# Packed attention and SoLU: w_out's column sums on TensorE from the shifted bits, a fourth load buffer, and units placed anew

## The chip, the cores and the metric

One core of a Trainium2 chip runs the kernel. The metric is the device time of one execution in microseconds (us); lower is better. Beside whole executions there is one execution under the profiler, with the busy time of each engine: PE (TensorE), PEld (its weight loads), DVE (VectorE), ACT (ScalarE), POOL (GpSimd) and SP (SyncE, which here issues the DMAs).

## The reference

A two-step attention over packed queries p (8 batches, 8 heads, 576 rows, 64 columns a head, 32 packed rows) is followed by a layer with a SoLU and a norm:

```
def sm_attn(qq, kk, vv):
    s = scale * np.matmul(qq, kk.transpose(0, 1, 3, 2))
    s = s - np.max(s, axis=-1, keepdims=True)
    a = np.exp(s)
    a = a / (np.sum(a, axis=-1, keepdims=True) + 1e-09)
    return np.matmul(a, vv)
p_packed = sm_attn(p, k, v)
out = sm_attn(q, p_packed, p_packed)
...
x = out.transpose(0, 2, 1, 3).reshape(B * S, H * D)        # 4608 x 512
h = x @ w_in                                               # 512 x 1024
e = np.exp(h - h_max)
sm = e / (np.sum(e, axis=-1, keepdims=True) + 1e-09)
solu = h * sm
...
ln = (solu - mu) / np.sqrt(var + 1e-06) * g_ln
return (ln @ w_out).astype(np.float32)                     # 1024 x 512
```

w_in, w_out and g_ln enter through their raw words: w_in and w_out come as pairs of 32-bit words (64-bit floating point), which the kernel joins into float32 itself.

## The kernel before, in words

The work has two parts. The **setup** turns w_in into float32 and w_out into two float16 parts (wch and wcl, whose sum carries more digits than one). The **main part** goes over eight batches b; a batch has four tiles of 128 rows, and each pair of batches a fifth, shared one.

For each batch, `pack(b)` (L342 on) loads k and v, transposes k, forms the scores of p, a softmax and the packed rows `ppT`. `unpack(b)` (L419 on) transposes q, forms its scores against `ppT`, a softmax over blocks of 32, and z, the product of the packed rows with w_in, as a high and a low part (`zh`, `zl`; L485 to L500); the attention's weights also become a high and a low part (`a2h`, `a2l`; L507, L508). In batch 0 the low part of z is made from a copy by ACT (L491) and a difference on POOL (L493); in later batches by one DVE step (L500).

For each tile, `mlp_in` forms h with 12 matmuls (24 for the shared tile; L521), its maximum on DVE (L523), the exponential on ACT (L531) and u on DVE (L534). `mlp_norm` makes `negmu` on POOL (L542), the two float16 parts `yhl` on ACT (L544) and DVE (L545), and a transposing DMA on SP's queue to `yT` (L547); tiny steps on POOL (L551 to L555) end in the row factor. `mlp_out` has 24 matmuls per tile (L564) with wch and wcl, and a DVE step (L566); SP stores the tile (L571).

In the setup, `high_part` (L195 on) takes a chunk's upper words: a pass on ACT scales them (L202, into a buffer 'e' of which there are two), DVE shifts the bits left by three and drops the sign (L204), and DVE puts the sign back (L205). `add_low_part` (L207 on) brings in the lower words, in the way that `HOW` names for each of eight chunks (0 to 3 of w_in, 4 to 7 of w_out, of 1024 columns each): a power from DVE (L212); then either one DVE step (L217; ways 0, 2, 6) or an ACT pass (L220) and a product on POOL (1, 3) or DVE (4, 5) (L221); then the sum on POOL (1, 2, 4) or DVE (0, 5) (L233), or on PE (3, 6), where each half is a float32 matmul (L226) and a float32r one (L227), with a copy by ACT (L229, or L231, which also multiplies by g).

`prepare_w_out` (L284 on) also needs the sum down each column of g times the magnitude of w_out. For each of eight pieces of 512 columns ACT makes g times the absolute value of the high part (`mag`, float32r; L301), and a matmul with ones adds it to one PSUM tile (L302). From the sum DVE makes a power of two for each column (L307 to L311). Then each piece is multiplied by g (ACT, L321, where that has not been done), by the scale (L322, on the engine that `SCALED_BY` names: p for POOL, otherwise DVE), copied to float16 (L323, ACT) and its rest made (L330, on the engine of `REST_BY`). The pieces lie in the buffers that `yT` and `yhl` use later. The first `mlp_out` needs all pieces.

The order of the setup and batch 0 comes from a scheduler with a planned time for each instruction; `tc.high_priority(offset=...)` moves a group ahead or back, and lists such as `PACK0`, `W_IN`, `UNPACK0`, `W_OUT`, `PARTS`, `FIRST_BATCH` hold those offsets. From batch 1 on, PE keeps the order of the program, in which `LATER` tells how many units of `pack` and `unpack` stand between a tile's steps; the other engines still go by priorities. Each engine runs its own queue in order. `keep_busy` (L251 on) puts filler matmuls (L255) into PE's queue, as many as `BUSY` says. `LOADS` is the order of the first loads on SP's queue: w a chunk of w_in, o one of w_out, p and P the first and the remaining part of p, k, v, q those of batch 0. The large load buffers `raw` (three) serve k, q and two chunks of w_out in turn.

Of the kernel before, what the change touches and what calls it, by code (L numbers as in the profile page):

```python
# [21 lines left out]
PACK0 = [-350, 400, 2010, 365, -1000, 60, -2800, 200, 200]
W_IN = [[110, -260], [-3000, -210], [100, -3010], [20, 850]]
UNPACK0 = [-80, 350, -35, -110, -70, -25, 1965, 1025, 0]
W_OUT = [[190, -10, 1910], [20, -60, -925], [-50, 2000, 0], [3010, -385, -3000]]
SCALE_AT = -1060
CHUNKS = [6, 0, 7, 5, 1, 3, 4, 2]
PARTS = [100, -1160, -990, -200, -3010, -1050, 200, 200]
FIRST_BATCH = [[0, 0, 1, 1, 1, 2, 0, 2, 0, 2, 0, 0], [0, 1, 0, 0, 0, 4, 1, 1, 0, 0, 1, 1], [3, 0, 6, 0, 0, 0, 0, 0, 0, 0, 0, 0], [1000, 375], [0, -400, -50], 190]
# [9 lines left out]
def packed_attention_solu_kernel(ctx: ExitStack, tc: tile.TileContext, q: bass.AP, k: bass.AP, v: bass.AP, p: bass.AP, w_in: bass.AP, w_out: bass.AP, g_ln: bass.AP, out: bass.AP):  # L39
# [202 lines left out]
    minus_h = const.tile([P, P], F16, name='minus_h')  # L242
    nc.vector.tensor_scalar_mul(minus_h, ident, -1.0)
    minus_r = const.tile([P, P], F32R, name='minus_r')
    nc.vector.tensor_scalar_mul(minus_r, ident, -1.0)
# [38 lines left out]
    def prepare_w_out():  # L284


        wg = []
        mps = ps_o.tile([P, DM], F32, name='po')
        for n in range(NFC // 2):
# [5 lines left out]
            with tc.high_priority(offset=W_OUT[n][0]):  # L295
                anchor = high_part(wg[n], w_out_raw[n], 4 + n)
            with tc.high_priority(offset=W_OUT[n][1]):
                for i in range(2):
# [2 lines left out]
                    nc.scalar.activation(mag, wg[n][:, i * DM:(i + 1) * DM], AF.Abs, scale=g_sb[:, c:c + 1])  # L301
                    nc.tensor.matmul(mps, lhsT=ones, rhs=mag, start=c == 0, stop=c == NFC - 1)  # L302
            with tc.high_priority(offset=W_OUT[n][2]):
                add_low_part(wg[n], w_out_raw[n], 4 + n, g_sb[:, 2 * n:2 * n + 2])
        with tc.high_priority(offset=SCALE_AT):
# [5 lines left out]
            last = nc.vector.tensor_scalar_mul(inv, power, 2.0 ** (-14))  # L311
        for c in CHUNKS:
            with tc.high_priority(offset=PARTS[c]):
# [10 lines left out]
                if REST_BY[c] == 'e':  # L324
                    ps = ps_a.tile([P, 512], F32, name='pa')
                    nc.tensor.matmul(ps, lhsT=ident, rhs=w, start=True, stop=False)
                    nc.tensor.matmul(ps, lhsT=minus_h, rhs=wch[:, c], start=False, stop=True)
                    nc.scalar.copy(wcl[:, c], ps)
                else:
                    EN(nc, REST_BY[c]).tensor_tensor(out=wcl[:, c], in0=w, in1=wch[:, c], op=ALU.subtract)  # L330
        return last.ins
# [87 lines left out]
    def unpack(b):  # L419
# [57 lines left out]
        for n in range(2):  # L477
# [6 lines left out]
            for r, pz in enumerate(banks):  # L484
                nc.scalar.copy(z_h[:, r, cols], pz)  # L485
                if b == 0:
                    if ZL_BY[2 * n + r] == 'd':
                        nc.vector.tensor_tensor(out=z_l[:, r, cols], in0=pz, in1=z_h.bitcast(F32)[:, r, cols], op=ALU.subtract)
                    else:
                        z = mlp.tile([P, 512], F32, name='o_sb', bufs=2)  # L490
                        nc.scalar.copy(z, pz)  # L491
                        if ZL_BY[2 * n + r] == 'p':
                            nc.gpsimd.tensor_tensor(out=z_l[:, r, cols], in0=z, in1=z_h.bitcast(F32)[:, r, cols], op=ALU.subtract)  # L493
                        else:
                            rest = ps_a.tile([P, 512], F32, name='pa')
                            nc.tensor.matmul(rest, lhsT=ident, rhs=z, start=True, stop=False)
# [193 lines left out]
```

## Time and profile before

| | |
|---|---|
| time, three runs | 471.25 us (median; 470.44 to 472.5) |
| the profiled execution | 472.61 us, span 470.8 us |
| granted clock of PE, mean | 0.967 of full speed |
| PE busy | 430.8 us (92% of the span) |
| DVE busy | 350.5 us (74%) |
| ACT busy | 232.3 us (49%) |
| POOL busy | 147.1 us (31%) |
| first output matmul (L564) | at 108.9 us |
| DMA | 67.0 MB, mean 142 GB/s |

The span runs from the first to the last instruction. Busy times are sums over one execution; the idle time of an engine costs something only where the end waits for it. A row of a group gives the line, the engine, the operation with out<-in, the count, the busy time, the mean of one in ns, and then the idle time of the engine just before and what ended it. A row of one line's or tile's instructions gives the shortest, median and longest duration in ns, and the first and last start in us. A row of the timeline or of the chain that ended last begins with the start and the duration in us.

### The profile page before, as it was taken

Reading aid. Unit: us, or ns where it says so; the run is one execution under the profiler, and the core shown is the slowest. Engines: PE = TensorE matmul, PEld = TensorE weight load, DVE = VectorE, ACT = ScalarE, POOL = GpSimd, SP = SyncE. Lnnn points to the kernel's source line nnn. Section 1 sums busy time; section 2 is a strip of 40 time slices with the busy share of each in tenths; the row PEclk is TensorE's granted clock in tenths of the full one; section 3 lists DMA queues with packets and bytes.
Section 4 is the critical chain, followed back from the end, with each engine's and each line's share of the span. In section 5 each row is a group of like instructions: output and inputs, shape, how many; then the busy total and the mean of one; then the engine's idle time right before and its main releaser. Section 6 shows DMA issues by size and latency. Waiting matters only on the chain.

```text
span 470.8 us, 8265 instructions
## 1 busy us (share of the span) xinstructions
PE 430.8 (92%) x3116; PEld 234.4 (50%) x3116; DVE 350.5 (74%) x648; ACT 232.3 (49%) x404; POOL 147.1 (31%) x244
## 2 busy tenths in 40 slices
PE   9698695859979999999999999999999989999995
PEld 7472243633534555446644654566446536575552
DVE  3568979778769887997489879984898587655551
ACT  3577748654344463546245544562447344433430
POOL 3424656936103311431124114310332142211220
PEclk9979859888999999999999999999999999999999
DMA  9999998999579979968949495447233413525342
GB/s 257 338 274 290 149 205 118 130 208 148 104 151 173 165 120 202 159 140 137 220 71 165 98 206 101 98 100 173 51 84 68 92 45 90 112 67 130 73 101 77
DMA packets 237880, 67.00 MB, mean 142 GB/s; under 512 B 208912, under 2 KB 231440, under 8 KB 237328
## 3 DMA queue, kind: packets, MB, share of 16 engines
q1 hardware_dynamic: 237840, 66.48, 74.2%
q8 instruction: 24, 0.39, 0.4%
q14 instruction: 16, 0.13, 0.1%
HBM read 37.23 MB, written 9.44 MB: 99 GB/s over the span
## 4 chain that ended last, share of the span: by engine, by line
PE 42%; DVE 28%; POOL 7%; ACT 6%; issue 6%; DMA 6%; SPq 5%; DVEq 0%; ACTq 0%; POOLq 0%
PE po L564 21%; PE h L521 12%; DVE nm L523 4%; DMA zh<-in_moe_w_in_dram 3%; DVE u L534 3%; DVE qT L428 3%; DVE kT L350 3%; PE pa L407 3%; DVE yhl L545 2%; DVE zl L500 2%; ACT yhl L544 2%; SPq L134 2%; DMA raw<-in_k_dram 2%; ACT e L381 1%; DVE a2l L508 1%
## 5 line engine op out<-in xcount | busy, mean ns | idle before, releaser
L564 PE MATMUL po<-wch,yT 128*128 128x512 f16 x576 | 178.2, 380 | 1.2 <-DMA yT<-yhl 1.2
L564 PEld LDWEIGHTS <-yT 128*128 128x128 f16 x864 | 80.9, 98 | 113.0 <-issue 18.4
L564 PE MATMUL po<-wcl,yT 128*128 128x512 f16 x288 | 108.7, 379 | 0.0
L521 PE MATMUL h<-zh,a2h 128*128 128x512 f32 x160 | 69.3, 433 | 1.7 <-DVE u L534 1.7
L531 ACT ACTIVATE e<-h,nm 128x1024 f32<-128x1024 f32 x36 | 39.9, 1109 | 59.4 <-DVE nm L523 59.4
L544 ACT ACTIVATE yhl<-u,negmu 128x1024 f16<-128x1024 f32 x36 | 41.4, 1149 | 49.7 <-POOL negmu L542 49.2
L521 PE MATMUL h<-zh,a2l 128*128 128x512 f32 x160 | 64.6, 404 | 0.3 <-DVE a2l L508 0.3
L521 PE MATMUL h<-zl,a2h 128*128 128x512 f32 x160 | 63.9, 400 | 0.6 <-POOL zl L493 0.6
L523 DVE TENSOR_REDUCE nm<-h 128x1 f32<-128x1024 f32 x36 | 43.9, 1220 | 23.6 <-PE h L521 23.5
L545 DVE SCALAR_TENSOR_TENSOR yhl<-u,negmu,yhl 128x1024 f16<-128x1024 f32 x36 | 46.4, 1288 | 17.5 <-ACT yhl L544 17.3
L534 DVE SCALAR_TENSOR_TENSOR u<-e,s_row,h 128x1024 f32<-128x1024 f32 x36 | 45.6, 1267 | 8.6 <-ACT e L531 7.4
L551 POOL TENSOR_SCALAR s_eps<-se,s_row 128x1 f32<-128x1 f32 x36 | 10.8, 301 | 121.7 <-ACT e L531 80.5
L566 DVE SCALAR_TENSOR_TENSOR o_sb<-po,c_row,inv 128x512 f32<-128x512 f32 x36 | 26.6, 738 | 22.6 <-PE po L564 22.6
L549 ACT ACTIVATE e<-u,negmu 128x1024 f32<-128x1024 f32 x36 | 40.9, 1137 | 3.4 <-POOL negmu L542 3.4
L554 POOL TENSOR_SCALAR c_row<-sq,s_eps 128x1 f32<-128x1 f32 x36 | 17.7, 492 | 79.4 <-ACT e L549 79.3
L521 PEld LDWEIGHTS h<-zh,a2h 128*128 128x128 f32 x160 | 31.0, 193 | 16.5 <-issue 7.9
L521 PEld LDWEIGHTS h<-zh,a2l 128*128 128x128 f32 x160 | 30.8, 192 | 9.0 <-DVE a2l L508 1.3
L521 PEld LDWEIGHTS h<-zl,a2h 128*128 128x128 f32 x160 | 30.8, 193 | 7.1 <-POOL zl L493 0.9
L485 ACT CAST zh<-pa 128x512 fp32r<-128x512 f32 x28 | 15.1, 583 | 26.1 <-PE pa L483 26.1
L444 POOL TENSOR_TENSOR s<-s,mx 128x576 f32<-128x576 f32 x14 | 15.9, 1158 | 36.9 <-DVE mx L443 36.9
L381 ACT ACTIVATE e<-pa,nmx 128x288 f32<-128x288 f32 x28 | 13.8, 497 | 26.9 <-DVE nmx L373 26.9
L483 PE MATMUL pa<-w_in_sb,ppT 64*32 64x512 f32 x224 | 19.9, 631 | 2.6 <-DVE zl L500 2.6
(138 smaller groups left out, 603.8 us busy)
## 6 DMA issues: line engine op xcount, KB each, us to landing
out_dram<-o_sb SPq DMA_DIRECT2D x36, 256.0 KB, 2.4
v_sb<-in_v_dram SPq DMA_DIRECT2D x16, 512.0 KB, 6.0
raw<-in_k_dram SPq DMA_DIRECT2D x28, 288.0 KB, 6.5
raw<-in_q_dram SPq DMA_DIRECT2D x96, 72.0 KB, 2.7
zh<-in_moe_w_in_dram SPq DMA_DIRECT2D x2, 1024.0 KB, 6.8
zl<-in_moe_w_in_dram SPq DMA_DIRECT2D x2, 1024.0 KB, 8.4
raw<-in_q_dram SPq DMA_DIRECT2D x4, 512.0 KB, 9.3
raw<-in_moe_w_out_dram SPq DMA_DIRECT2D x2, 1024.0 KB, 6.5
```

What stands on the lines that cost most here:

```text
L381: nc.scalar.activation(dst, src, AF.Exp, bias=nmx, accum_out=es[:, n:n + 1])
L483: nc.tensor.matmul(banks[r][32 * g:32 * g + 32, :], lhsT=ppT[rows, 32 * g:32 * g + 32], rhs=w_in_sb[rows, g, cols], start=True, stop=True)
L521: nc.tensor.matmul(h[:, 512 * n:512 * n + 512], lhsT=lhsT, rhs=z[:, r, 512 * n:512 * n + 512], start=t == 0, stop=t == len(terms) - 1)
L523: nc.vector.tensor_reduce(out=nm, in_=h, axis=AX.X, op=ALU.max, negate=True)
L531: nc.scalar.activation(e, h, AF.Exp, bias=nm, accum_out=se)
L534: nc.vector.scalar_tensor_tensor(out=u, in0=e, scalar=s_row, in1=h, op0=ALU.mult, op1=ALU.mult, accum_out=su)
L544: nc.scalar.activation(yhl[:, 0], u, AF.Identity, bias=negmu)
L545: nc.vector.scalar_tensor_tensor(out=yhl[:, 1], in0=u, scalar=negmu, in1=yhl[:, 0], op0=ALU.add, op1=ALU.subtract)
L549: nc.scalar.activation(e, u, AF.Square, bias=negmu, accum_out=sq)
L554: nc.gpsimd.tensor_scalar(out=c_row, in0=sq, scalar1=1.0 / DF, scalar2=s_eps, op0=ALU.mult, op1=ALU.add)
L564: nc.tensor.matmul(po, lhsT=yT[:, a, c], rhs=w[:, c], start=c == 0 and t == 0, stop=c == NFC - 1 and t == 2)
L566: nc.vector.scalar_tensor_tensor(out=o_sb, in0=po, scalar=c_row, in1=inv, op0=ALU.mult, op1=ALU.mult)
```

## The change

1. The column sums are formed from the shifted bits that `high_part` leaves (the magnitude of the high part before the sign is put back), as float32, with g's magnitude as the weights, one column repeated 128 times. The ACT passes and the tile `mag` go.
2. `raw` has four buffers. The place comes from tiles that now share others: p's first part goes to a buffer of `ppT`, the scratch of p's remaining part to the tiles `a2h1` and `a2l1`, and two constants (`minus_h`, `minus_r`) go, with two ways of making a rest on PE that no list named.
3. p's remaining part (P) is loaded behind all of w_out.
4. Steps go to other engines (`HOW`, `SCALED_BY`, `REST_BY`, `ZL_BY`, `A2L_BY`), and groups get other offsets and places. `YT_BY` and `STORE_BY` are new, and name SP throughout, as before.

```
-HOW = '14313324'
-SCALED_BY = 'pppppdpp'
-REST_BY = 'pdddppdd'
-ZL_BY = 'pppp'
-A2L_BY = 'dd'
+HOW = '22136326'
+SCALED_BY = 'spsdssdd'
+REST_BY = 'pdddpddd'
+ZL_BY = 'pppd'
+A2L_BY = 'dp'
...
-LOADS = 'wpkwvwwqooPoo'
-BUSY = [[8, 100], [6, 0], [0, -3000], [0, -100], [2, -190], [0, -485], [4, 200], [2, -2885], [28, 285], [134, -20], [26, 20], [64, 50]]
+LOADS = 'wpkwvwwqooooP'
+BUSY = [[0, -75], [10, -3070], [0, 200], [0, -410], [0, 1950], [0, -80], [8, -100], [0, -215]]
...
-        raw = raws.tile([P, G, NB, 32], F32, name='raw', bufs=3)
+        raw = raws.tile([P, G, NB, 32], F32, name='raw', bufs=4)
...
-    pT0 = const.tile([P, G, J], F32, name='pT0')
+    pT0 = att.tile([P, G, J], F32, name='ppT', bufs=2)
...
-                raw = raws.tile([P, NP2, J], F32, name='p2raw')
+                raw = par.tile([P, 2 * (S + LEFT)], F32, name='a2h1')[:, :NP2 * J].rearrange('p (x j) -> p x j', j=J)
...
-        return nc.vector.scalar_tensor_tensor(out=dst.bitcast(I32), in0=hi, scalar=-2147483648, in1=bits, op0=ALU.bitwise_and, op1=ALU.bitwise_or)
+        nc.vector.scalar_tensor_tensor(out=dst.bitcast(I32), in0=hi, scalar=-2147483648, in1=bits, op0=ALU.bitwise_and, op1=ALU.bitwise_or)
+        return bits.bitcast(F32)
...
-        t = raws.tile([P, NP2 * J], F32, name='p2t')
+        t = par.tile([P, 2 * (S + LEFT)], F32, name='a2l1')[:, :NP2 * J]
...
+        g_abs = const.tile([P, NFC], F32, name='g_abs')
+        nc.scalar.activation(g_abs, g_sb, AF.Abs)
...
-                anchor = high_part(wg[n], w_out_raw[n], 4 + n)
+                mag = high_part(wg[n], w_out_raw[n], 4 + n)
...
-                    mag = mlp.tile([P, DM], F32R, name='mag', bufs=1)
-                    nc.scalar.activation(mag, wg[n][:, i * DM:(i + 1) * DM], AF.Abs, scale=g_sb[:, c:c + 1])
-                    nc.tensor.matmul(mps, lhsT=ones, rhs=mag, start=c == 0, stop=c == NFC - 1)
+                    nc.tensor.matmul(mps, lhsT=g_abs[:, c:c + 1].broadcast_to([P, P]), rhs=mag[:, i * DM:(i + 1) * DM], start=c == 0, stop=c == NFC - 1)
```

In `LATER` the units of `pack` and `unpack` stand at other places between the tiles' steps, and the offsets become, for the first of its three rows,

```
-[-20, 100], [0, -190, 1000], 0]
+[670, -40], [0, -1000, 0], 0]
```

where the first pair is the priority of `unpack` and of `pack`, and the second triple the lag, the priority of `mlp_out` and that of `mlp_norm`.

More of the change, by code (lines that the diff above doesn't have):

```diff
@@ L16 @@
 U_MAX = 2.0 ** 14
-HOW = '14313324'
-SCALED_BY = 'pppppdpp'
-REST_BY = 'pdddppdd'
-ZL_BY = 'pppp'
-A2L_BY = 'dd'
[L22 to L29, printed above, removed]
@@ new lines @@
+SCALED_BY = 'spsdssdd'
+REST_BY = 'pdddpddd'
+ZL_BY = 'pppd'
+A2L_BY = 'dp'
+PACK0 = [-20, -200, 250, -110, -100, -100, -75, 400, 20]
+W_IN = [[50, 45], [-210, 50], [825, -200], [1000, -50]]
+UNPACK0 = [2025, 2000, 1975, 1850, -20, -20, -825, -3000, 1000]
+W_OUT = [[435, 10, 1985], [940, 3000, -940], [3155, -400, 2000], [-200, -75, -25]]
+SCALE_AT = -850
+CHUNKS = [3, 0, 6, 1, 5, 2, 7, 4]
+PARTS = [-290, 75, 75, 75, 75, -20, 2060, -20]
+FIRST_BATCH = [[0, 0, 3, 1, 0, 2, 1, 1, 0, 0, 0, 1], [1, 1, 0, 0, 0, 0, 0, 1, 0, 2, 1, 3], [6, 3, 0, 0, 0, 0, 0, 0, 0, 0, 0, 0], [-30, -20], [0, -520, -20], 405]
@@ L33 @@
+LOADS = 'wpkwvwwqooooP'
+LATER = [[[4, 0, 1, 0, 0, 1, 0, 0, 1, 0, 0, 0], [0, 0, 0, 0, 2, 0, 0, 1, 0, 2, 3, 1], [0, 0, 0, 0, 0, 0, 0, 0, 0, 0, 0, 0], [670, -40], [0, -1000, 0], 0], [[3, 1, 0, 0, 0, 1, 0, 0, 1, 0, 0, 1], [0, 0, 0, 0, 0, 0, 2, 1, 0, 2, 3, 1], [0, 0, 0, 0, 0, 0, 0, 0, 0, 0, 0, 0], [645, -50], [0, -1000, 0], 0], [[4, 0, 0, 2, 0, 1, 0, 0, 0, 0, 0, 0], [1, 0, 0, 1, 1, 0, 0, 1, 2, 0, 0, 3], [0, 0, 0, 0, 0, 0, 0, 0, 0, 0, 0, 0], [620, -50], [0, -1000, 0], 0]]
 FETCH = [[['k', 0, 0], ['v', 0, 0], ['q', 0, 0]], [['k', 0, 0], ['v', 0, 0], ['q', 0, 0]], [['k', 0, 0], ['v', 0, 0], ['q', 0, 0]]]
+BUSY = [[0, -75], [10, -3070], [0, 200], [0, -410], [0, 1950], [0, -80], [8, -100], [0, -215]]
@@ L35, in EN @@
+YT_BY = 'ssssssssss'
+STORE_BY = 's'
 def EN(nc, c):
@@ L99, in load_x @@
     def load_x(src):
-        raw = raws.tile([P, G, NB, 32], F32, name='raw', bufs=3)
+        raw = raws.tile([P, G, NB, 32], F32, name='raw', bufs=4)
         load_blocks(raw, src)
@@ L109, in load_rows @@
     def load_rows(src):
-        raw = raws.tile([P, G, NB, 32], F32, name='raw', bufs=3)
+        raw = raws.tile([P, G, NB, 32], F32, name='raw', bufs=4)
         flat = raw.rearrange('p g a i -> p (g a i)')
@@ L178, in packed_attention_solu_kernel @@
             if tag == 'r':
-                raw = raws.tile([P, G * NB * 32], I32, name='raw', bufs=3)[:, :2 * DF]
+                raw = raws.tile([P, G * NB * 32], I32, name='raw', bufs=4)[:, :2 * DF]
             else:
@@ L241, in packed_attention_solu_kernel @@
     nc.vector.tensor_copy(ident_r, ident)
[L242 to L245, printed above, removed]
     for _ in range(12):
@@ L310, in prepare_w_out @@
             nc.vector.tensor_scalar(out=scale.bitcast(I32), in0=power.bitcast(I32), scalar1=-1, scalar2=254 + 14 << 23, op0=ALU.mult, op1=ALU.add)
-            last = nc.vector.tensor_scalar_mul(inv, power, 2.0 ** (-14))
+            nc.vector.tensor_scalar_mul(inv, power, 2.0 ** (-14))
         for c in CHUNKS:
@@ L323, in prepare_w_out @@
                 nc.scalar.copy(wch[:, c], w)
[L324 to L331, printed above, removed]
+                EN(nc, REST_BY[c]).tensor_tensor(out=wcl[:, c], in0=w, in1=wch[:, c], op=ALU.subtract)
     def pair(b):
@@ L491, in unpack @@
                         nc.scalar.copy(z, pz)
[L492 to L496, printed above, removed]
-                            nc.tensor.matmul(rest, lhsT=minus_r, rhs=z_h[:, r, cols], start=False, stop=True)
-                            nc.scalar.copy(z_l[:, r, cols], rest)
+                        nc.gpsimd.tensor_tensor(out=z_l[:, r, cols], in0=z, in1=z_h.bitcast(F32)[:, r, cols], op=ALU.subtract)
                 else:
@@ L546, in mlp_norm @@
         yT = mlp.tile([P, 2, NFC, P], F16, name='yT', bufs=2)
-        nc.sync.dma_start(yT.rearrange('p t c n -> p (t c) n'), yhl.rearrange('p t f -> p (t f)'), transpose=True)
+        queue = nc.scalar if YT_BY[min(row // P, 9)] == 'a' else nc.sync
+        queue.dma_start(yT.rearrange('p t c n -> p (t c) n'), yhl.rearrange('p t f -> p (t f)'), transpose=True)
         sq = small.tile([P, 1], F32, name='sq')
```

3 lines of the change are left out of this document (1 added, 2 removed).

## The prediction

> **What bounds the kernel now.** I read the page first, then the busy time cut into the kernel's own stages, then who waited for whom in the worst stages, then the chain that ended last.
>
> ```profile
> span 470.8 us, 8265 instructions
> PE 430.8 (92%) x3116; PEld 234.4 (50%) x3116; DVE 350.5 (74%) x648; ACT 232.3 (49%) x404; POOL 147.1 (31%) x244
> ```
> ```profile
> 0.00:38.00 38.00, 32.52 (x328) 23.77 (x329) 18.98 (x37) 21.22 (x40) 13.09 (x16) 0.91 1.02 275
> 38.00:62.00 24.00, 17.07 (x77) 5.62 (x76) 23.28 (x30) 19.45 (x30) 14.20 (x7) 0.91 1.16 237
> 62.00:72.00 10.00, 9.69 (x47) 4.79 (x50) 6.70 (x9) 2.35 (x9) 4.52 (x3) 0.54 1.23 182
> 72.00:97.00 25.00, 18.24 (x201) 13.43 (x202) 22.36 (x39) 16.97 (x35) 21.39 (x19) 0.93 1.06 125
> 97.00:109.00 12.00, 7.04 (x55) 2.70 (x56) 9.54 (x20) 6.98 (x11) 3.44 (x10) 0.72 1.06 220
> 109.00:160.00 51.00, 46.79 (x353) 22.02 (x351) 40.16 (x79) 21.91 (x40) 15.81 (x21) 1.00 0.91 143
> 160.00:450.00 290.00, 283.79 (x2006) 155.33 (x2005) 223.01 (x430) 139.93 (x240) 72.65 (x165) 1.00 0.62 118
> 450.00:470.80 20.80, 15.68 (x72) 6.78 (x70) 6.48 (x10) 3.48 (x5) 1.99 (x5) 0.99 0.37 88
> ```
> Columns: stretch, length, then busy time of PE, PE's weight loads, DVE, ACT, POOL, the granted clock, the DMA share and GB/s. From 160 to 450 us TensorE is busy 283.8 of 290: that part is PE work at full clock, and an edit on another engine can win at most the 6.2 us of gaps. The tail's 5.1 us of idle is the last tile's chain, which the change leaves alone. So what can move is the ramp. PE is idle 6.9 us from 38 to 62 (DVE full: 23.3 of 24), 6.8 us from 72 to 97 (POOL 21.4 and DVE 22.4 of 25) and 5.0 us from 97 to 109, just ahead of the first output matmul; and its clock is 0.54 from 62 to 72 and 0.72 from 97 to 109.
>
> The waits from 72 to 110 us name the holders:
> ```profile
> PE h L125 <- ACT qT L129: 5.1, 2, 2.9
> POOL yT L322 <- DVE o_sb L310: 4.9, 1, 4.9
> PE pa L467 <- DVE s L439: 4.7, 1, 4.7
> ...
> PE h L521 <- DVE u L534: 1.7, 2, 1.5
> ```
> The three PE rows add up to 11.5 us, that is nearly all of the 6.8 + 5.0. Behind them stands POOL, as the chain that ended last shows:
> ```profile
> 67.56 2.36 POOL yT L233
> ...
> 74.87 1.38 POOL yT L322
> 76.25 2.89 POOL yhl L322 x2
> ...
> 86.22 2.68 POOL wcl L330 x2
> ...
> 96.81 0.20 POOL negmu L542
> ...
> 108.92 4.86 PE po L564 x22
> ```
> From 75 to 97 us the chain lies almost wholly on POOL, which works through the scaling of w_out's chunks (four of its pieces are shown); a tile's tiny negmu, for which ACT and then DVE wait, stands in that queue.
>
> **The change, part by part.** The profiled execution took 472.61 us for a span of 470.8; the median of the three runs is 471.25, 1.4 lower. I make the sum against the former and apply the difference to the latter.
>
> *The column sums.* The eight ACT passes that make g times the magnitude go, and the sum reads the shifted bits, with g as weights, in plain float32 instead of the rounded float32r.
> ```profile
> L301 ACT ACTIVATE mag<-yT,g_sb x4: 716/728/746, 36.5 to 53.6; 128x512 fp32r<-128x512 f32 x4
> ```
> ```profile
> 35.10 0.86 PE pa L226 x2
> 35.96 0.24 PE pa L227
> ```
> ACT loses 8 x 0.73 = 5.8 us and gets one 128x8 pass (bounds 0.1 to 0.7, taken 0.2). The two chain rows are a float32 and a float32r matmul of the same 128x512 shape: 0.86 (in two instructions) against 0.24. So PE gains 8 x 0.62 = 5.0 us. The weights are now one column repeated 128 times; no row shows such a load, and I bound it between no more than an ordinary one (hidden beside the matmul before) and 8 x 0.2 = 1.6 us on PE; I take nothing. What a sum waited for was DVE's sign step, ACT's pass and PE's place; now only the shift. The last one ran late for another reason:
> ```profile
> 61.91 0.75 ACT L301 ACTIVATE mag<-yhl,g_sb 128x512 fp32r<-128x512 f32 x1
> ...
> 70.31 0.80 PE L302 MATMUL po<-mag,ones 128*128 128x512 f32 x1
> ```
> Its ACT input was written by 62.7, so 7.6 us of that was its place in PE's queue. The 4.9 us that POOL waited for the scale (L310) come from there. If the sums are placed earlier, that wait goes; what is late next is chunk 6's low part (POOL's L233 at 67.6 to 69.9), which leaves a gain of a few us only. The added wait: a buffer of 'e' is now free only when PE has summed it, and the ACT pass at L202 of the chunk after next waits for that. Queued behind it on ACT are the copies of qT, the exponentials of the first softmax and the copies of z, and DVE's bit steps wait for L202.
>
> *The low parts (HOW) and the scaling (SCALED_BY, REST_BY, ZL_BY, A2L_BY).* By kind, before to after: ACT's L220 7 to 3, POOL's L221 5 to 3, POOL's L233 5 to 4, DVE's product (L221 or L217) 3 to 5, chunks that add on PE 3 to 4, ACT's L321 4 to 0, POOL's L322 7 to 1, DVE's 1 to 7, POOL's L330 3 to 2, DVE's 5 to 6, one zl from ACT's copy and POOL (L493) to one DVE step, one a2l from DVE to POOL.
> ```profile
> L220 ACT ACTIVATE u<-zh x4: 1128/1144/1157, 7.1 to 72.6; 128x1024 f32<-128x1024 uint32 x2, 128x1024 fp32r<-128x1024 uint32 x2
> ```
> ```profile
> L221 POOL TENSOR_TENSOR u<-u x5: 2344/2515/3071, 10.5 to 54.0; 128x1024 fp32r<-128x1024 f32 x3, 128x1024 f32<-128x1024 f32 x2
> L221 DVE TENSOR_TENSOR u<-u x2: 1224/1664/2105, 18.9 to 75.2; 128x1024 f32<-128x1024 f32 x2
> ```
> ```profile
> L322 POOL TENSOR_TENSOR yhl<-yhl,o_sb x4: 1272/1496/2253, 76.2 to 92.9; 128x512 f32<-128x512 f32 x4
> ...
> L322 DVE TENSOR_TENSOR yT<-yT,o_sb x1: 1760/1760/1760, 77.3 to 77.3; 128x512 f32<-128x512 f32 x1
> ```
> ```profile
> L330 DVE TENSOR_TENSOR wcl<-yhl,wch x4: 676/865/2577, 82.9 to 94.9; 128x512 f16<-128x512 f32 x4
> L330 POOL TENSOR_TENSOR wcl<-yT,wch x3: 1158/1160/1567, 86.2 to 89.0; 128x512 f16<-128x512 f32 x3
> ```
> ```profile
> L493 POOL TENSOR_TENSOR zl<-o_sb,zh x4: 1267/1534/1793, 56.6 to 62.4; 128x512 fp32r<-128x512 f32 x4
> ```
> POOL sheds 2 x 2.5 + 2.4 + 6 x 1.5 + 1.2 + 1.5 = 19.1 us and takes one a2l (by L493's row for nine eighths of its size, 1.7): net -17.4. ACT's further loss, 4 x 1.1 in L220 and 4 x 0.7 (by L301's row, the same pass) in L321, stands against two half copies after PE. DVE's step of this size costs 0.68 undisturbed (676 in L330) and up to 2.58 when held up, so DVE takes on 6 x 0.68 + 2 x 1.22 + 2 x 0.68 - 0.75 = 7.1 us, while it sheds what POOL's steps held it up.
>
> Now what lies on the path.
> ```profile
> 93.70 0.08 DVE L534 DVE_READ_ACCUMULATOR u<-e,s_row,h 128x1 f32 x1
> ```
> (a) PE's 5.1 us behind ACT's qT copies: these stood behind L220 and L321 passes and behind casts of wch that waited for the scaling. ACT keeps the copies and the casts, so I take half: -2.6 (bounds 0 to -5.1). (b) PE's 4.7 us behind L439: that DVE step stood behind a yhl step, that behind ACT, that behind negmu at 96.81, though DVE had that tile's sum ready at 93.8. POOL then has one L322 instead of seven, and negmu can come 2.9 us earlier: -2.9 (0 to -4.7). (c) 38 to 62 us: POOL's 14.2 us lose about half (one L221, one L233, one L493), and with them half of what DVE was held up, against chunk 4's product and a zl that come to DVE: -0.6 (-2 to +1). (d) DVE's own addition from 72 to 97: seven L322 and one more L330 at 0.68 against the L322 of 1.76 and L221 of 2.1 that go, +1.6, of which the 2.6 us of DVE's idle time there hide some: +1.0 (0 to +4). (e) PE: +5.0 for sums, +2.2 for one more chunk that adds on PE (two float32 and two float32r matmuls), -1.0 for four filler matmuls fewer (22 to 18, 0.24 each) = 6.2 us, placed where PE idles 6.9 us between 38 and 62; if that cover were gone it would cost all 6.2. I charge +1.0.
>
> *Loads.* SP's queue now issues w_out's last two chunks ahead of the rest of p:
> ```profile
> 27.57 7.00 SPq L167 DMA_DIRECT2D p2raw<-in_p_dram  x4
> ```
> They come 7 us sooner. p's consumer (pack of batch 1) begins only when k of batch 1 is there, behind the same bytes in both orders, so this costs nothing; its scratch now lies in the second pair of a2 tiles, whose zero pads POOL writes after the scratch has been read: if POOL reaches them before that transfer has landed, everything on POOL waits. Bounds 0 to +3, taken 0. The fourth buffer lets k and q of later batches wait less, but through the ramp SP issues without a break at a DMA share near 1, so I take 0 (0 to -2).
>
> *The order of units (LATER, UNPACK0 and the like).* Same instructions, other places. After 160 us the bounds are the 6.2 us of gaps on one side and as much again on the other; nothing in the profile favours a side, so 0.
>
> Sum: -2.6 - 2.9 - 0.6 + 1.0 + 1.0 = -4.1. The profiled execution would be 468.5, the median 467.1; I forecast 467.
>
> [...] Clock first:
> ```profile
> 24.00:30.00 6.00, 5.95 (x41) 4.59 (x41) 3.81 (x8) 4.19 (x9) 2.42 (x1) 0.50 0.98 224
> ...
> 60.00:72.00 12.00, 11.62 (x52) 5.41 (x58) 8.70 (x12) 4.35 (x13) 5.37 (x3) 0.57 1.18 190
> ```
> In both PE is full and slow, and the second follows PE's idle patches of 38 to 62. [...] Then: DVE's lone L322 took 1.76 and one L330 2.58 where another took 0.68, all while POOL was busy. [...]
>
> **Rivals.**
> *The clock stays up.* The longer matmuls fill the idle patches, and 60 to 72 us run at full clock: 12 x (1 - 0.57) = 5.2 us, less what then waits for DVE, say 4.5 more than forecast: 462.5. For it, PE is the full engine from 62 to 72; against, DVE is nearly full just before. 15%.
> *SP holds the first output.* The first yT transpose stood behind other loads:
> ```profile
> 90.27 1.29 DVE L545 SCALAR_TENSOR_TENSOR yhl<-u,negmu,yhl 128x1024 f16<-128x1024 f32 x1 [1.56 <-ACT yhl L544]
> ```
> ```profile
> 89.19 8.45 SPq L85 DMA_DIRECT2D raw<-in_q_dram  x11
> ...
> 100.13 5.83 SPq L547 DMA_TRANSPOSE yT<-yhl  x2
> ```
> Tile 0's yhl was written by 91.6. If that order stays, (b) and most of (a) are lost and the start at 108.9 moves little: 470.5. 18%.
> *DVE is held up.* The moved steps cost half-way to 1.76: 7 x 0.54 = 3.8 more: 470.9. Against: POOL has little left to hold them with. 7%.
> *PE becomes the bound of the ramp: slower.* The sums hold the 'e' buffers and stand ahead of z's and the first tile's matmuls, so the 6.2 us lie on the path and only half of (a) and (b) is won, too late: 471.25 + 6.2 - 2.7 = 474.8, rounded up to 475 for the half clock. It decides once PE has no idle time left between 38 and 72. 13%.
>
> **The numbers.** The forecast itself has 47%. The range runs from 459 (clock rival with the better bounds of a and b) to 474.5 (into the slower rival); about 15% is left out. A difference of 0.5%, 2.4 us, is what a measurement can tell from none. Faster than that, below 468.9: 0.41 of the forecast's 0.47, the clock's 0.15 and 0.02 of the SP case, 0.58. Within: 0.06 + 0.16 + 0.06 = 0.28. Slower: 0.14.
>
> **What would show it.** Right: POOL's busy time down by about 17 us and ACT's by about 12; PE's matmul records up by some 10; no L322 on POOL but one; the last sum before 62 us; the first output matmul at 102 to 106 us instead of 108.9; PE idle from 72 to 109 near 6 us; 160 to the end unchanged within 2 us. Wrong: first output matmul at 108 or later with SP's loads ahead of the first yT (SP rival); clock near 1 from 60 to 72 (clock rival); ACT waiting at L202 for PE, or PE without gaps from 38 to 72 and the first h matmul later than 57 us (slower); or a gain or loss that lies after 160 us, which nothing here foresees.

## The result and the profile after

The kernel after takes 479.24 us (median of six runs, 478.0 to 480.52), the kernel before 472.03 beside it (470.44 to 472.55): a ratio of 1.0157, 95% interval 1.0133 to 1.0181. It is slower by 7.2 us where 4 us less were forecast, and outside the range.

The page's first lines and the table by stage, of after (columns as in the prediction):

```profile
span 477.8 us, 8259 instructions
...
PE 435.4 (91%) x3126; PEld 236.7 (50%) x3126; DVE 356.4 (75%) x655; ACT 220.6 (46%) x390; POOL 132.0 (28%) x234
```
```profile
38.00:62.00 24.00, 19.56 (x95) 7.16 (x95) 22.36 (x32) 12.34 (x19) 12.91 (x6) 0.86 1.16 213
62.00:72.00 10.00, 6.36 (x45) 3.87 (x47) 10.00 (x18) 3.26 (x7) 2.33 (x2) 0.82 1.12 164
72.00:97.00 25.00, 22.17 (x203) 14.60 (x202) 23.78 (x45) 17.32 (x37) 8.23 (x14) 0.86 1.00 132
97.00:109.00 12.00, 3.86 (x27) 1.72 (x26) 4.14 (x11) 3.29 (x5) 2.65 (x8) 0.75 1.05 153
109.00:160.00 51.00, 45.53 (x327) 20.82 (x326) 36.02 (x69) 16.52 (x32) 9.55 (x14) 0.79 1.07 164
160.00:450.00 290.00, 285.59 (x2032) 156.09 (x2031) 229.99 (x436) 141.73 (x244) 77.00 (x167) 1.00 0.61 114
```
From 160 us to the end PE is idle 9.5 us, in before 11.3, so the loss lies in front of 160 us. From 72 to 97 PE is busy 3.9 us more than in before, as meant; then, from 97 to 109, it is busy for 3.9 us of 12 where before was for 7.0, and from 109 to 160 its clock is 0.79 instead of 1.00. The row maxima on DVE of the fourth tile (tile 3), of the shared fifth tile and of the ninth tile in order of time mark where the loss lies, first before, then after:

```profile
100.74 1.22 DVE L523 TENSOR_REDUCE nm<-h 128x1 f32<-128x1024 f32 x1
...
126.32 1.23 DVE L523 TENSOR_REDUCE nm<-h 128x1 f32<-128x1024 f32 x1 [1.14 <-PE h L521]
...
177.07 1.23 DVE L523 TENSOR_REDUCE nm<-h 128x1 f32<-128x1024 f32 x1 [0.30 <-PE h L521]
```
```profile
97.20 1.22 DVE L509 TENSOR_REDUCE nm<-h 128x1 f32<-128x1024 f32 x1
...
142.43 1.23 DVE L509 TENSOR_REDUCE nm<-h 128x1 f32<-128x1024 f32 x1 [0.79 <-PE h L507]
...
186.45 1.23 DVE L509 TENSOR_REDUCE nm<-h 128x1 f32<-128x1024 f32 x1 [0.30 <-PE h L507]
```
After is 3.5 us ahead at 97 us, near the forecast's 4.1, and 16.1 us behind at the fifth tile. Part of these 16.1 is only order, since after has 72 output matmuls behind it there and before 44. At the ninth row maximum both have 144 output matmuls behind them, and the rest of PE's work is the same in both: there after is 9.4 us behind, so the ramp lost 12.9 us. From there to the end it is 2.4 us quicker than before (291.4 us for 293.8). SP's queue in between (start, duration, x: DMAs), and two rows of DVE and ACT:

```profile
81.74 6.45 SPq L98 DMA_DIRECT2D raw<-in_k_dram  x4
88.70 10.72 SPq L87 DMA_DIRECT2D raw<-in_q_dram  x16
99.52 2.19 SPq L98 DMA_DIRECT2D raw<-in_k_dram  x2
101.80 4.52 SPq L534 DMA_TRANSPOSE yT<-yhl  x1
106.43 1.15 SPq L109 DMA_DIRECT2D v_sb<-in_v_dram  x2
```
```profile
89.13 1.27 DVE L531 SCALAR_TENSOR_TENSOR yhl<-u,negmu,yhl 128x1024 f16<-128x1024 f32 x1
```
```profile
108.07 1.15 ACT L530 ACTIVATE yhl<-u,negmu 128x1024 f16<-128x1024 f32 x1 [8.35 <-DMA yT<-yhl]
109.12 0.48 ACT L373 ACTIVATE e<-pa,nmx 128x288 f32<-128x288 f32 x1
```
Tile 0's `yhl` is written at 90.4, but its transposing DMA is issued at 101.8, behind 18 loads for batches that come much later, and lands at 108. ACT's third `yhl` waits 8.35 us for that landing, since `yhl` has two buffers, and holds the exponentials of batch 2's packing (L373) behind it. Now PE, after and then before:

```profile
99.26 0.69 PE L360 MATMUL pa<-kT,pT 64*32 64x288 f32 x8
108.09 0.61 PE L551 MATMUL po<-wch,yT 128*128 128x512 f16 x1 [8.14 <-DMA yT<-yhl]
...
115.93 0.71 PE L459 MATMUL pa<-qT,ppT 64*32 64x288 f32 x16
...
121.00 0.72 PE L459 MATMUL pa<-qT,ppT 64*32 64x288 f32 x16
```
```profile
96.96 0.72 PE L467 MATMUL pa<-qT,ppT 64*32 64x288 f32 x16
102.40 1.55 PE L467 MATMUL pa<-qT,ppT 64*32 64x288 f32 x16 [4.71 <-DVE s L439]
...
108.85 0.39 PE L564 MATMUL po<-wch,yT 128*128 128x512 f16 x1
```
Before has the same late yT (issued at 100.1, first output matmul at 108.9), but batch 1's scores (L467) stand ahead of the output matmuls in PE's queue. After has them behind 24 and 44 output matmuls, so all of batch 1's softmax, z and the fifth tile wait for that DMA. (Behind the 8.14 us of idle the f16 matmul above takes 0.61 us, and the granted clock is 0.50 from 108 to 112 us; before's takes 0.39, with the clock at 1.00 from 108.85 to 112.)

### The profile page after: what moved, and what is told of

Same layout as the page of the kernel before. It is cut to its first block, busy times and chain, and to the rows that moved or that the text cites. A ratio compares the mean times of both kernels' runs of the same rounds, so it can differ in the third digit from the quotient of the medians.

```text
span 477.8 us, 8259 instructions
## 1 busy us (share of the span) xinstructions
PE 435.4 (91%) x3126; PEld 236.7 (50%) x3126; DVE 356.4 (75%) x655; ACT 220.6 (46%) x390; POOL 132.0 (28%) x234
## 4 chain that ended last, share of the span: by engine, by line
PE 60%; DVE 19%; DMA 8%; SPq 7%; issue 3%; ACT 2%; POOL 1%; DVEq 0%; ACTq 0%
PE po L551 31%; PE h L507 19%; DMA zh<-in_moe_w_in_dram 3%; DMA yT<-yhl 2%; PE pa L459 2%; SPq L87 2%; SPq L169 2%; PE pa L475 2%; PE pa L399 2%; PE pa L389 2%; PE pa L360 2%; DVE kT L342 2%; DVE nm L509 2%; DVE qT L420 2%; DVE yhl L531 2%
## 5 line engine op out<-in xcount | busy, mean ns | idle before, releaser
L551 PE MATMUL po<-wch,yT 128*128 128x512 f16 x576 | 180.9, 383 | 9.4 <-DMA yT<-yhl 9.4
L551 PE MATMUL po<-wcl,yT 128*128 128x512 f16 x288 | 110.0, 383 | 0.0
L507 PE MATMUL h<-zh,a2h 128*128 128x512 f32 x160 | 70.5, 441 | 4.1 <-ACT a2h L493 3.8
L531 DVE SCALAR_TENSOR_TENSOR yhl<-u,negmu,yhl 128x1024 f16<-128x1024 f32 x36 | 47.9, 1330 | 19.2 <-ACT yhl L530 19.1
L538 POOL TENSOR_SCALAR s_eps<-se,s_row 128x1 f32<-128x1 f32 x36 | 9.5, 265 | 115.1 <-ACT e L517 57.0
L373 ACT ACTIVATE e<-pa,nmx 128x288 f32<-128x288 f32 x28 | 13.7, 496 | 20.1 <-DVE nmx L365 20.1
L389 PE MATMUL pa<-ident,e 128*128 128x128 f32 (+1 forms) x80 | 14.4, 307 | 7.3 <-ACT e L373 6.9
```

Source lines behind the costliest of these rows:

```text
L389: nc.tensor.transpose(out=pt[:n, i * P:(i + 1) * P], in_=e1[:, r, cols], identity=ident)
L507: nc.tensor.matmul(h[:, 512 * n:512 * n + 512], lhsT=lhsT, rhs=z[:, r, 512 * n:512 * n + 512], start=t == 0, stop=t == len(terms) - 1)
L531: nc.vector.scalar_tensor_tensor(out=yhl[:, 1], in0=u, scalar=negmu, in1=yhl[:, 0], op0=ALU.add, op1=ALU.subtract)
L551: nc.tensor.matmul(po, lhsT=yT[:, a, c], rhs=w[:, c], start=c == 0 and t == 0, stop=c == NFC - 1 and t == 2)
```

## The experiments

Four theories: A, SP's queue holds the first yT. B, the float32 sums cost PE more than was charged. C, the places in `LATER`. D, PE's order, batch 0's output matmuls ahead of batch 1's scores. A fifth came from the runs: P, the place of the buffers in memory.

| run | us (lowest to highest) | ratio to before beside it, 95% |
|---|---|---|
| after | 479.24 (478.0 to 480.52) | 1.0157 (1.0133 to 1.0181) |
| e1_yt_act | 488.0 (483.71 to 488.76) | 1.0347 (1.030 to 1.0394) |
| e2_three_raw | 487.49 (487.11 to 488.31) | 1.0357 (1.034 to 1.0374) |
| e3_before_sums | 483.47 (481.6 to 485.06) | 1.0281 (1.0243 to 1.0319) |
| e4_old_later | 483.21 (482.28 to 485.16) | 1.0269 (1.0239 to 1.030) |
| e5_gate | 482.0 (481.13 to 482.87) | 1.0219 (1.0199 to 1.0239) |
| e6_sp_order | 522.43 (519.57 to 524.49) | 1.1072 (1.1029 to 1.1115) |
| e7_gate_sp | 515.73 (512.53 to 518.4) | 1.0932 (1.0878 to 1.0985) |
| e8_sums_gate | 480.92 (480.76 to 481.98) | 1.0204 (1.0186 to 1.0222) |
| e9_hold | 472.65 (471.97 to 473.35) | 1.002 (1.0004 to 1.0036) |
| e10_hold_gate | 469.99 (468.8 to 470.8) | 0.9958 (0.9942 to 0.9974) |
| e11_before_hold | 477.68 (476.77 to 478.31) | 1.0113 (1.0078 to 1.0148) |
| e12_shift | 466.08 (465.23 to 466.42) | 0.9883 (0.9864 to 0.9901) |
| e13_hold_still | 476.08 (475.91 to 476.37) | 1.0099 (1.0082 to 1.0117) |
| e14_before_shift | 468.9 (467.5 to 468.98) | 0.994 (0.9924 to 0.9956) |
| e15_at_128 | 471.56 (469.12 to 475.16) | 0.9998 (0.9968 to 1.0027) |
| e16_at_64 | 478.2 (477.21 to 479.45) | 1.0138 (1.0112 to 1.0164) |
| e17_shift_gate | 472.09 (471.24 to 473.44) | 1.0007 (0.9994 to 1.0021) |
| e18_sums_placed | 479.93 (478.39 to 480.52) | 1.0171 (1.0144 to 1.0197) |

Before itself took 470.8 to 472.2 us beside these groups of runs, so a difference between runs of two groups is uncertain by about 1 us.

**One part undone.**

```
e1:  -YT_BY = 'ssssssssss'     +YT_BY = 'aaaaasssss'
e2:  -  name='raw', bufs=4)    +  name='raw', bufs=3)
e3:  before, with g_abs and the matmul with g_abs and mag in place of L300 to L302
e4:  LATER as in before
```


> The changed kernel, with the first five tiles' yT transposes issued from ACT's queue instead of SP's. Theory A (SP's queue holds the first output): the first yT is issued within 2 us of its yhl (written at 90.4 us in the changed kernel, where the transfer was issued at 101.8), the first output matmul starts at 95 to 98 us instead of 108.1, and the time falls by the 8.1 us gap and some 2 us of the half clock behind it, to 467 to 472 us. Theory B (the float32 sums cost PE time and clock) and theory C (the units of later batches stand in worse places): the first output comes sooner, but PE's lost time turns up elsewhere and the time stays at 476 us or more.

> The changed kernel with three load buffers again instead of four, nothing else. SP's order then has 11 of the 16 loads of q of batch 3 ahead of the first yT, and none of k of batch 4; the last chunk of w_out is loaded ahead of k of batch 1. Theory A: five q loads of 0.67 us and two k loads of 1.1 us less ahead of yT let the first output start 4 to 6 us sooner, and the time falls to 472 to 476 us. Theories B and C: the fourth buffer has no part in the loss, 478 to 481 us.

> The kernel before, with the column sums alone done anew (from the shifted bits, float32, g's magnitude as weights), and nothing else. Theory B: PE's 5.0 us more and a held buffer of e make it slower by 3 to 6 us, 475 to 478 us. Theory A: 12 loads of q instead of 11 stand ahead of the first yT and the sums lie in PE's idle time, so it stays within 2 us of the kernel before, 470 to 474 us.

> The changed kernel with the places and priorities of later batches' units (LATER) as in the kernel before. Theory C: the half clock of 130 to 140 and 150 to 157 us goes and the time falls by 4 us or more, to 475 us or less. Theory A: SP's order ahead of the first yT is the same as in the changed kernel, so the gap of 8 us stays and the time is 477 to 481 us.

None came out as A or B had it. In e1 ACT issued the first yT only at 97.65, and it still took 6.6 us to land beside the loads. In e2 the ready list of the scheduler (what it may place next) put the setup in another order, and PE waited 7.5 us at one matmul of a low part (L230) for DVE: not a clean test. e3 was slower by 12.7 us, and its PE queue too now had output matmuls (24) ahead of batch 1's scores. e4 was slower than after, with the same 24 and 44 output matmuls ahead of the two halves of the scores: C falls. This put PE's order in question.

**The gate.** One 18-column matmul on batch 1's softmax maxima ahead of the first output puts batch 1's scores ahead of all output matmuls.

```
             nc.vector.tensor_reduce(out=mx, in_=s2[r], axis=AX.X, op=ALU.max)
+            seen[b] = mx
...
         po = ps_o.tile([P, DM], F32, name='po')
+        if row == 0:
+            nc.tensor.matmul(po[:NB, :NB], lhsT=seen[1], rhs=seen[1], start=True, stop=True)
```


> The changed kernel, with one tiny matmul (18 columns) ahead of the first tile's output matmuls that reads the row maxima of batch 1's scores, so that PE's queue holds batch 1's scores and most of its z (L459, L475) ahead of all output matmuls, as in the kernel before; SP's order up to the first yT stays that of the changed kernel. Theory D (PE's queue spends the output matmuls of batch 0 ahead of batch 1's scores, and nothing is left to cover that batch's softmax): batch 1's scores start near 99 us instead of 115.9, h of the shared tile starts near 120 instead of 134, and the time falls by 6 us or more, to 473 us or less. Theory A (SP's queue holds the first yT): that transfer is issued at 101 to 102 us as in the changed kernel, so the time stays within 2 us of 479.

> The kernel before with the new column sums alone, as run above at 483.5 us, and the tiny matmul that puts batch 1's scores ahead of the output matmuls in PE's queue. Theory D: what the sums cost there was the place of the outputs, so the time falls by 8 us or more, to 475 us or less. Theory B (the float32 sums cost PE time and clock): it stays at 480 us or more.

D alone isn't it: e5 stayed above 480 us, and e8 came out where B had it. The waits in e5, from 95 to 125 us, show why:

```profile
ACT yhl L532 <- DMA yT<-yhl: 11.8, 2, 7.8
...
PE pa L461 <- ACT e L374: 9.2, 1, 9.2
```
Batch 1's scores (L461), both halves, need the PSUM buffers `pa` that batch 2's exponential (L374) still reads, and that stands on ACT behind the `yhl` that waits for yT. SP's hold reaches PE by another way. In e8 the gate won 2.5 us of e3's loss (3.6 if each is taken against before beside it), where D asked for 8.

Two runs gave SP its program's order (`EngineType.SP` added to the engines of `manual_schedule`, q's loads at a later tile), without and with the gate:

> The changed kernel, with SP's queue in the order of the program in the main part, k and v of batch b+2 at a batch's first tile and q at its fourth (batch 0) or third: no load of batch 3 or 4 stands ahead of the first yT. PE's order is that of the changed kernel, output matmuls ahead of batch 1's scores. Theory A: the first yT is issued within 3 us of its yhl, the first output starts at 94 to 98 us and the time falls to 467 to 472 us. Theory D: batch 1's scores still stand behind 24 output matmuls, the gap comes behind the third output instead, and the time falls by half of that at most, 474 to 478 us.

They took 522 and 516 us (for e7 469 or less was expected if A and D hold): the loads then came late, in e6 q of the fourth batch at 168.93 us and k of the fifth at 181.72, where after has them at 88.70 and 99.52. The first yT moved to 97.4, but no theory is tested by that.

**Loads held back.** q of the fourth batch and k of the fifth, whose loads stood ahead of yT, wait for the third tile's halves; in e11 the same is done to before.

```
+    mark = const.tile([P, 1], F32, name='mark')
...
+        if row == 256:
+            nc.gpsimd.tensor_copy(mark, yhl[:, 1, :1])
...
+        if held:
+            nc.gpsimd.tensor_copy(raw[:, :, 0:1, :1], mark.unsqueeze(1).unsqueeze(2).broadcast_to([P, G, 1, 1]))
```


> The kernel after, with the load of q of the fourth batch and of k of the fifth made to wait on SyncE's queue for the third tile's halves: GpSimd copies one column of the third tile's yhl (L531) and writes it into one element of each 32x32 block row of the load buffer before the load, which overwrites it. The first transposing DMA (L534) then stands ahead of these 18 loads. The added work is three small GpSimd instructions. The ready list then also puts 9 of the first 24 output matmuls (L551) ahead of batch 1's last packing matmul and all 48 of the first two tiles ahead of the second half of batch 1's scores (L459). Theory A (SyncE's queue is what costs): yT issued near 91 and landed near 96 instead of 101.8 and 108.0, TensorE's 8.1 us behind it gone, batch 1's first softmax maximum (L435, 125.2 in after) at 117 or sooner, time 466 to 473. Theory D (what costs is that batch 0's output matmuls are spent ahead of batch 1's scores, so that TensorE runs short while batch 1's softmax chain runs): the early yT is spent as early, softmax maximum not before 120, the fifth tile's row maximum (L509) after 138, half clock between 130 and 160, time 476 to 482.

> The kernel after with the held loads of the run before (q of the fourth batch and k of the fifth behind the third tile's halves) and with the gate: one 18-column matmul on the maxima of batch 1 ahead of the first output, which puts batch 1's scores (L459) and three quarters of its z (L475) ahead of all output matmuls. The transposing DMA is early, so ScalarE isn't held at yhl (L530) and batch 1's exponential of pack comes in time. If A and D are each half of the loss: softmax maximum of batch 1 at 103 to 110, the fifth tile's row maximum at 126 to 132, time 463 to 470. If A alone is the loss, it equals the run without the gate within 1 us. If neither is (something else in the ramp, for example the work that TensorE does at half clock), 476 to 482.

> The kernel before with the same held loads (its SyncE queue too has 11 loads of q of the fourth batch and v of the third ahead of the first yT, written at 91.6, issued at 100.1). The sums stay as they were. The ready list then puts 24 output matmuls between the two halves of batch 1's scores and 17 more ahead of its z. Theory A: yT issued near 97 instead of 100.1, behind v alone; time 468 to 471, at most that of before. Theory D: the second half of batch 1's scores stands behind 24 output matmuls that wait for yT, so batch 1's softmax maximum comes after 107.6 by the time of that wait and of 24 matmuls (5 us and more): time 474 to 480, slower than before although its yT is sooner.

The first looks like A, the second like A and D, the third like D. But e9 and e10 were 2.2 us ahead before any held load: the constant `mark` had moved every later buffer up by 32 bytes. Three runs part the two edits:

> The kernel after with one more 4-byte column in the constants (and GpSimd's copy into it, of one column of the third tile's halves), but no load held. It moves every later buffer up by 32 bytes, as in the two runs with held loads, where the opening ran 2.2 us ahead of after's (fourth w_in chunk's conversion at 24.40 instead of 26.57). Each queue's order is that of after. If the addresses made the opening faster: the same 24.4, yT still issued near 100, time 476 to 478. If the opening was sooner for another reason: 26.6 and 478.5 to 480. Theory A needs in both cases that it stays above 475.

> The held loads (q of the fourth batch and k of the fifth behind the third tile's halves), with the mark kept in the first column of g_abs, which the sums have done with, so that no buffer moves. Theory A alone, without the shift: opening as in after (26.6), first yT issued near 91 instead of 101.8; time 473.5 to 476, which is the time of after less 3.5 to 5. If the 32 bytes made the whole gain of the first run with held loads: 478 or more.

> The kernel before with 64 more bytes in the constants, so that its load buffers begin at a multiple of 256 bytes, as they do in the run of after with the extra column (those of before begin 192 beyond one, those of after 224 beyond one). If the place in the 256 bytes is what made the opening faster: the fourth w_in chunk's conversion 2 us sooner than 26.48, and a time 1 to 2 us under before's. If not: no difference (within 0.8 us).

The shift alone takes after to 466.08, 13.2 us less and below every expectation. Its SP queue, PE queue and two row maxima:

```profile
79.45 9.03 SPq L87 DMA_DIRECT2D raw<-in_q_dram  x16
88.58 1.98 SPq L100 DMA_DIRECT2D raw<-in_k_dram  x2
90.65 3.71 SPq L541 DMA_TRANSPOSE yT<-yhl  x1
```
```profile
97.12 0.69 PE L365 MATMUL pa<-kT,pT 64*32 64x288 f32 x8
97.75 0.39 PE L558 MATMUL po<-wch,yT 128*128 128x512 f16 x1
...
103.03 0.72 PE L464 MATMUL pa<-qT,ppT 64*32 64x288 f32 x16
...
108.10 0.72 PE L464 MATMUL pa<-qT,ppT 64*32 64x288 f32 x16
```
```profile
78.59 1.21 DVE L514 TENSOR_REDUCE nm<-h 128x1 f32<-128x1024 f32 x1
...
129.40 1.22 DVE L514 TENSOR_REDUCE nm<-h 128x1 f32<-128x1024 f32 x1 [0.66 <-PE h L512]
```
Every queue has after's order (GpSimd's has the one copy more), and the engines' own steps take as long as in after (medians within 3%, but for one group of setup matmuls); only the loads are faster, so SP's queue reaches the first yT 11.2 us sooner, 2.4 us behind `yhl` (88.3) instead of 11.4. Tile 0's row maximum is 2.6 us sooner (78.59 for 81.19), batch 1's scores and the fifth tile 12.9 and 13.0. PE's rows part the 12.9: the last matmul ahead of the outputs (L365, after's L360) starts 2.1 us sooner, which is the opening's loads; the gap of 8.1 us is gone (8.2 from that matmul to the first output); and the 24 outputs up to the scores take 5.3 us where after, slow behind its gap (the 0.50 above), takes 7.8. So 10.8 us came with yT. (From 109 to 160 us e12's clock is 0.83, little above after's 0.79: most of that slow stretch is not the loss.) In before the same cure (e14) also issues yT 6.0 us sooner (94.13), but its ramp moves by the opening's 3.1 us alone (fifth tile 123.12 for 126.32) and its time by 2.5: there nothing but the output waits for yT. With both moved, after beats before, 466.08 to 468.9. The ninth row maximum, first e12, then e14, shows where:

```profile
173.44 1.22 DVE L514 TENSOR_REDUCE nm<-h 128x1 f32<-128x1024 f32 x1 [0.32 <-PE h L512]
```
```profile
173.85 1.22 DVE L525 TENSOR_REDUCE nm<-h 128x1 f32<-128x1024 f32 x1 [0.30 <-PE h L523]
```
At tile 3's row maximum e12 was 2.6 us ahead of e14 (95.08 for 97.67), here it is only 0.4 ahead, and the other 2.4 of the 2.8 come behind it, with the same work left in both.

e13 shows A without a shift: yT at 91.0, but the ready list used it to put 48 output matmuls ahead of batch 1's first scores (110.84); it wins 3.2 us. The same order is in e9, whose first scores come at 107.98 although its yT is sooner than e12's: with fast loads the hold costs 6.6 us (472.65 to 466.08). e11's buffers lay 224 bytes beyond a multiple of 256 and its order changed, so it settles nothing by itself.

**Which place.** In the compiled programs all buffers behind the constants begin equally far beyond a multiple of 256 bytes (each large one is a multiple of 256 long). The constants' sizes give the differences between the offsets in the table below; the traces hold no addresses.

```
     packed = {}
+    pad = const.tile([P, 40], F32, name='pad')      (e15; 24 in e16, 8 in e18)
+    nc.gpsimd.memset(pad, 0.0)
```


> The kernel after with 160 more bytes in the constants: every later buffer, which in after begins 224 bytes beyond a multiple of 256, then begins 128 beyond one (0 in the run shifted by 32 bytes, 192 in before). Orders are after's. If transfers want their buffers on multiples of 128: opening as in the shifted run (the fourth chunk of w_in at 24.4, near 348 GB/s), 465 to 468. If only multiples of 256 do: the opening at 26.5 and near 290 GB/s, 470 or more.

> The kernel after with 96 more bytes in the constants: every later buffer begins 64 beyond a multiple of 256, on a multiple of 64 but not of 128, as those of before do (192). If 64 is enough: 465 to 468. If 128 or 256 is wanted but 64 is better than 32: the opening as in before (near 290 GB/s, 26.5), first yT between 92 and 100, 468 to 475. If 64 is no better than 32: 477 or more.

DMA issues of after, e12 and e15 (KB each, median us from issue to landing):

```profile
v_sb<-in_v_dram SPq DMA_DIRECT2D x16, 512.0 KB, 6.3
raw<-in_k_dram SPq DMA_DIRECT2D x28, 288.0 KB, 6.7
...
yT<-yhl SPq DMA_TRANSPOSE x36, 4.4
```
```profile
v_sb<-in_v_dram SPq DMA_DIRECT2D x16, 512.0 KB, 5.4
raw<-in_k_dram SPq DMA_DIRECT2D x28, 288.0 KB, 4.7
...
yT<-yhl SPq DMA_TRANSPOSE x36, 3.7
```
```profile
v_sb<-in_v_dram SPq DMA_DIRECT2D x16, 512.0 KB, 5.9
raw<-in_k_dram SPq DMA_DIRECT2D x28, 288.0 KB, 4.6
...
yT<-yhl SPq DMA_TRANSPOSE x36, 4.4
```

| kernel | bytes beyond a multiple of 256 | k's loads, us | first yT issued | time |
|---|---|---|---|---|
| after | 224 | 6.7 | 101.80 | 479.24 |
| after, e16 | 64 | 6.5 | 101.27 | 478.2 |
| after, e15 | 128 | 4.6 | 95.89 | 471.56 |
| after, e12 | 0 | 4.7 | 90.65 | 466.08 |
| before | 192 | 6.5 | 100.13 | 472.03 |
| before, e14 | 0 | 4.5 | 94.13 | 468.9 |

k's loads come in pieces of 128 bytes that lie 128 bytes apart. In the table's runs they took 4.5 to 4.7 us at 0 and 128, where no piece lies across a multiple of 256, and 6.5 to 6.7 at 64, 192 and 224, where every second piece does. v's loads, in pieces of 512 bytes, took 5.3 to 5.4 us at 0, where a piece fills two stretches of 256, and 5.9 to 6.3 at 64, 128, 192 and 224, where it touches three. What a transfer does at such a multiple no trace shows. e15's opening is 0.5 us sooner than after's, e12's 2.2 to 2.3. In after's four kernels the time follows the first yT: 11.2 us of issue, 13.2 us of time.

**What remains.**

> The kernel after with the 32 bytes and with the gate (batch 1's scores and three quarters of its z ahead of all output matmuls), loads not held. Theory D, with place and queue cured: TensorE runs less short behind batch 1's softmax, 2 to 3 us off the shifted run's time, as with the held loads: 463 to 465. If the softmax chain no longer binds once yT is in time: 466 to 469, no gain or a loss.

> The kernel before with the new sums alone, as in the run that took 12.7 us longer than before, but with 32 more bytes, so that its buffers begin on multiples of 256 (there, 224 beyond one, as in after). If the place made most of those 12.7 us: 468 to 473, beside 468.9 for before with its buffers moved there. If the float32 sums or the order that they bring cost the most (theories B and D): 475 to 480.

With yT in time the gate costs 6.0 us (472.09, outside both expectations). The stretch from 97 to 109 us, e12 and then e17:

```profile
97.00:109.00 12.00, 12.00 (x87) 4.80 (x87) 6.16 (x13) 5.10 (x10) 3.23 (x7) 1.00 1.29 242
```
```profile
97.00:109.00 12.00, 7.12 (x52) 1.31 (x56) 10.96 (x19) 5.91 (x11) 3.72 (x7) 0.64 0.93 187
```
PE is busy 7.1 of 12 us, because the outputs that filled it in e12 (12.0 of 12) must wait. So "scores first" isn't the better order in itself: behind the held loads (e9, with 48 outputs ahead of the scores) the same gate won 2.7 us. What decides it is not shown. e18 keeps an 11.0 us loss against e14, as B and D had it: place made only 3.5 of e3's 12.7 (4.9 if each is taken against before beside it). There PE's order puts the scores at 104.41 (e14: 93.89), and tile 0's row maximum comes 3.9 us later (72.90 for 68.96), but tile 3's only 0.8 (98.49 for 97.67), so most of the loss arises behind tile 3. How B and D share the 11 us stays open.

## Why the prediction was wrong, step by step

- *Counts.* Right: POOL -15.1 (said -17), ACT -11.7 (-12), PE's records +10, one L321 on POOL (before's L322), and the last sum before 62 us (the scale's first step starts at 61.95, before 71.2).
- *(a) to (e), sum -4.1.* Right in sum as far as 97 us: -3.5 at tile 3's row maximum. Tile 0's came 9.2 us later (81.19 for 72.04), and tiles 2 and 3 made up for it. One term was off inside: DVE's four L321 on `yhl` took 1.70 us in the median, not the 0.68 of (d); the rows stand below this list. That after takes 466.08 with the loads fast, near the forecast's 467, is luck: e12 has a gift of 2.1 to 2.6 us in its opening, and against before with its buffers moved alike only 0.4 us of the 4.1 are left at the ninth row maximum. The other 2.4 it wins behind 173 us, where 0 was forecast. Why 2.2 of the 2.6 us that e12 is ahead of e14 at tile 3 are gone by then stays open.
- *"Loads", the step that failed.* The fourth buffer was booked at 0 to -2 because SP "issues without a break". That was the reason to look for a cost: a yT that is ready sooner comes no sooner out of a full queue. Its wait there grew from 8.6 us to 11.4, which took all that (a) and (b) had won, and with what stands behind it on PE SP's queue cost 10.8 us where 0 was booked: 8.2 of standing still and 2.6 of slow matmuls. How much of the 18 loads ahead is the fourth buffer's doing stays open, since e2 changed the setup's order as well.
- *"The order of units", 0.* It also failed. It looked only past 160 us. In the ramp PE's new order put batch 1's scores behind 24 output matmuls, which made a late yT, harmless in before, the start of a chain. The sum had no term for this. Which part of the change brought that order is not isolated: the old `LATER` keeps it (e4), and in before the new sums alone bring it (e3).
- *The SP rival.* The right mechanism, at 18%, with the wrong price: 470.5 assumed that only (a) and (b) are lost with the first output matmul. It came at 108.09, SP's loads ahead of yT, just as its sign said. What was missing was the list of what is queued on PE behind that matmul. PE's idle time from 72 to 109, forecast near 6 us, was 11.0 (11.7 in before).
- *PE becomes the bound of the ramp.* Its sign was there (first h matmul at 64.75 for 57.4), its mechanism wasn't the loss: e12 has the same sums and placements at 466.08.
- *The clock stays up.* From 62 to 72 the clock was 0.82, not near 1 (before 0.54), and PE was busy for only 6.4 of the 10 us, so this rival did not come true. That idle patches set the clock there was the author's estimate from before's stretch alone; no run parts it from the rest.
- *160 to the end unchanged within 2 us.* Narrowly missed: behind the ninth row maximum the new order of units wins 2.4 us.

The steps that moved to DVE, in after, and a step of POOL beside the last of them:

```profile
L321 DVE TENSOR_TENSOR yhl<-yhl,o_sb x4: 771/1698/1887, 67.5 to 76.8; 128x512 f32<-128x512 f32 x4
```
```profile
71.18 0.68 DVE L321 TENSOR_TENSOR yT<-yT,o_sb 128x512 f32<-128x512 f32 x1
...
76.78 1.89 DVE L321 TENSOR_TENSOR yhl<-yhl,o_sb 128x512 f32<-128x512 f32 x1
```
```profile
76.27 1.84 POOL L494 TENSOR_TENSOR a2l<-s,a2h 128x576 fp32r<-128x576 f32 x1
```
Of the five L321 and six L323 on DVE, three and one took 1.64 to 1.89 us. These four are the ones that began while a two-input step of POOL was under way (its own L321 or L323, or the a2l that the change moved there); the others took 0.64 to 0.77. So the delay of the rival in which DVE is held up came true, at about 4 us of DVE's time, but tile 3's row maximum was on time even so.

## What to carry to other kernels

When a DMA feeds the engine that bounds the kernel, list what stands ahead of it on its queue and what stands behind its consumer on the consumer's queue: the second list tells whether a late transfer costs anything. Before's first transposed tile waited 8.6 us and held up nothing but the outputs; after's waited 11.4 and cost 10.8. And look up where buffers begin after any change to the constants: 32 bytes moved this kernel by 2.7%, more than the change did, so compare two versions with their buffers placed alike.

## What the runs showed of the hardware that was not expected

- k's loads, in 128-byte pieces, took 4.5 to 4.7 us at 0 or 128 bytes beyond a multiple of 256 and 6.5 to 6.7 at 64, 192 and 224 (the table's runs); a 64-byte multiple was no help (e16, 6.5).
- The transposing DMA from SBUF to SBUF also gained, at 0 only: 3.7 us there (e12, e14), 4.3 to 4.4 at 64, 128, 192 and 224.
- DVE's L321 and L323, with two inputs in SBUF, took 1.64 to 1.89 us when they began during a two-input step of POOL, and 0.64 to 0.77 us else (after, 67 to 81 us).
- e15 spread over 6.0 us (469.12 to 475.16) in twelve runs, e12 over 1.2; why was not tried.
